# Attention with an MLP behind it on one core: tail exponentials added to the row sums by accumulating transfers, the sums' product half a pair later with half its passes

## The chip, the cores and the metric

One core of a Trainium2 chip runs the whole kernel. The metric is the device time of one execution in microseconds, as the median of several runs. Engines are TensorE (PE, its weight loads PEld), VectorE (DVE), ScalarE (ACT), GpSimd (POOL) and SyncE (SP); DMA transfers are issued by SP and by POOL.

## What is computed

```python
# q, k, v: (4 batches, 12 heads, 448 positions, 64); w_in (768, 2048), w_out (2048, 768)
scores = cap * np.tanh(np.matmul(q, k.transpose(0, 1, 3, 2)) / sqrt(64) / cap)
attn = np.exp(scores - scores.max(axis=-1, keepdims=True))
attn = attn / (np.sum(attn, axis=-1, keepdims=True) + 1e-09)
x = heads side by side of np.matmul(attn, v)          # (1792, 768)
h = x @ w_in
P = a[0] + a[1] * h + a[2] * h * h + a[3] * h * h * h
Q = 1.0 + abs(b[0]) * abs(h) + abs(b[1]) * h * h
out = (P / (Q + 1e-6)) @ w_out
```

## The kernel before

**Steps and pairs.** Attention goes through 24 steps p, each with two heads (j = 0, 1) of one batch; two steps make a pair k. The 448 keys of a head are cut in four blocks n: three of 128 and a tail of 64. Scores stand transposed, keys in partitions and the 448 queries in columns. For n = 0, 1, 2 a tile holds both heads side by side (128 x 896). The two tails share one tile of 128 x 448: keys of the first head in partitions 0 to 63, of the second in 64 to 127. A step takes the blocks in the order 0, 1, 3, 2 (ORDER, line 56); m counts places in this order.

**What a step does.** `scores` (L417, and L316 for the tail) multiplies keys by queries into one of three PSUM tiles ps. ScalarE applies tanh in place (L429) and then the exponential (L449) into an SBUF tile: e for n < 3, et for the tail. The cap is bounded here, so no maximum is subtracted (the flag `bounded`; the other branch does not run). VectorE adds the three e tiles into es[p], first block 1, then block 2 (L455). At place m = 2 TensorE also transposes keys (into the PSUM bank mi, L335 and L337) and queries (L341) of step p + 2, and VectorE turns them into high and low halves (`convert_k`, L369 and L370; L361 and L364). The value product `pv` (L500) of step p - 1 comes in two parts: blocks 0 and 1 at m = 2 of step p, block 2 and the tail at m = 3. VectorE copies its result to U[p - 1] (L509).

**The sums' product.** `norm(k)` (L512 to L551) makes the sums over keys for the four heads of a pair: a product of a 128 x 32 block of ones with es, for each of two heads of two steps, then four more products that add the tails. A tail tile holds two heads, so its stationary operand is `half[j]`, ones in the 64 partitions of head j and zeros elsewhere:

```python
        for last in range(2):
            for j in range(2):
                for x in range(2):
                    h = 32 * (2 * j + x)
                    st, mv = (self.half[j], tails[x][0][:, 0]) if last else (self.ones, es[x][:, j])
```

The result stands in mi. VectorE copies it to DB (L533), four transfers put it in a tile of 32 x 56, VectorE adds the guard and takes the reciprocal (L542, L543), one transfer writes it to DRAM (dn), and two broadcast it over 128 partitions. `xout` (L562) multiplies U by it. All these transfers are GpSimd's except for the last pair, where they are SyncE's. `norm(p // 2 - 1)` is called at the end of m = 3 of each even step.

**What sets the order.** `Plan` collects operations with estimated costs (D_NS, line 58, is that of the sums' product) and what they read and write, and `flush` writes each engine's queue in the order in which they would start by these costs. Each engine works through its queue in order.

**Behind attention.** `split_x` turns six pieces of x (kc) in two halves m into a high and a low part. For m = 1 both are ScalarE's (L573, L579), and a transfer by GpSimd accumulates x on the low one. The MLP has stage 1 (L755, x times w_in, three products for each piece), a rational function on ScalarE and VectorE (L782 to L795, whose high and low halves are L794 and L795) and stage 2 (L820). The first two units of stage 1 need the pieces of m = 0 alone; the third and fourth need those of m = 1, which depend on the last steps' outputs.

## Time and profile before

| | |
|---|---|
| median of three runs (lowest, highest) | 699.83 us (698.43, 700.53) |
| the profiled execution: its time | 696.99 us |
| the profiled execution: span of the core | 695.2 us |
| mean granted clock of TensorE | 0.995 |
| busy: PE, PEld, DVE, ACT, POOL | 674.9, 545.4, 552.1, 450.1, 102.3 us |

A span runs from the first to the last instruction. Busy time is that of one engine's instructions; a busy TensorE need not be at its peak, as its matmuls are pipelined. A wait is put down to the engine whose signal came last. One fp32 product of TensorE shows as two records.

### The profile page before, as it was taken

The numbers are of one execution on the slowest core, as the hardware profiler recorded it, in microseconds if no ns is written. First come the engines' busy times: TensorE is split into PE (matmuls) and PEld (weight loads), VectorE is DVE, ScalarE is ACT, GpSimd is POOL, SyncE is SP. The second block draws the span as 40 slices with busy tenths as digits, with TensorE's granted clock in tenths as the row PEclk, the third lists the DMA queues.
The fourth block names the chain that finished last, engine by engine and source line by source line (L and its number), as shares of the span: only waits on it lengthen the run. The fifth ranks groups of instructions, "written<-read, shape, count | busy, mean of one in ns | idle before, by whom it ended". The sixth has DMA issues, their size and how long they took to land.

```text
span 695.2 us, 9792 instructions
## 1 busy us (share of the span) xinstructions
PE 674.9 (97%) x3781; PEld 545.4 (78%) x3781; DVE 552.1 (79%) x682; ACT 450.1 (65%) x551; POOL 102.3 (15%) x168
## 2 busy tenths in 40 slices
PE   6899999999999899999999999999999999999986
PEld 4554455445547799999999999999999999999986
DVE  4579998987864879767998688698689869778783
ACT  3788878888895796666557458546655744755520
POOL 4022232333222200011002001101100200110000
PEclk9999999999999999999999999999999999999999
DMA  6637666744224744267119316714821841681044
GB/s 147 144 97 208 173 144 130 166 108 109 55 74 81 132 143 153 66 135 140 46 51 170 76 51 153 137 45 89 185 68 45 146 106 46 137 206 67 23 180 166
DMA packets 81912, 79.95 MB, mean 115 GB/s; under 512 B 48960, under 2 KB 69184, under 8 KB 81856
## 3 DMA queue, kind: packets, MB, share of 16 engines
q1 hardware_dynamic: 70496, 53.74, 26.3%
q0 software_dynamic: 11360, 25.50, 20.6%
q8 instruction: 31, 0.51, 0.3%
q14 instruction: 25, 0.20, 0.1%
HBM read 50.73 MB, written 25.65 MB: 110 GB/s over the span
## 4 chain that ended last, share of the span: by engine, by line
PE 85%; DVE 5%; ACT 5%; DMA 2%; SPq 2%; issue 1%; DVEq 0%
PE ps L755 32%; PE ps L820 16%; PE pv L500 9%; PE mi L820 8%; PE pv L820 8%; PE ps L417 6%; PE mi L528 3%; PE ps L316 2%; ACT etiles L449 2%; ACT ps L429 2%; SPq L283 1%; PE ps L341 1%; PE mi L335 1%; DMA arena_r<-dn 1%; DVE arena_f L455 1%
## 5 line engine op out<-in xcount | busy, mean ns | idle before, releaser
L755 PE MATMUL ps<-arena_r,ring 128*128 128x512 f32 (+1 forms) x1152 | 249.2, 368 | 2.0 <-DMA arena_r<-arena_f 1.5
L755 PEld LDWEIGHTS ps<-arena_r,ring 128*128 128x128 f32 x1152 | 209.0, 188 | 28.7 <-DMA arena_r<-arena_f 1.9
L429 ACT ACTIVATE ps<-ps 128x896 f32<-128x896 f32 (+1 forms) x96 | 76.6, 817 | 33.2 <-PE ps L417 28.2
L820 PE MATMUL ps<-arena_r,etiles 128*128 128x384 f32 x462 | 90.3, 335 | 0.7 <-DVE etiles L795 0.7
L786 DVE SCALAR_TENSOR_TENSOR arena_f<-arena_f,bab 128x896 f32<-128x896 f32 x32 | 36.8, 1150 | 63.9 <-ACT arena_f L783 63.9
L782 ACT ACTIVATE arena_f<-ps,b 128x896 f32<-128x896 f32 x32 | 32.4, 1013 | 84.5 <-PE ps L755 84.3
L283 POOL DMA_DIRECT2D sums<-arena_f x42 | 36.5, 869 | 341.8 <-ACT arena_f L852 340.5
L820 PEld LDWEIGHTS ps<-arena_r,etiles 128*128 128x128 f32 x462 | 81.1, 188 | 2.2 <-DVE etiles L795 1.0
L449 ACT ACTIVATE etiles<-ps,acap 128x896 f32<-128x896 f32 (+1 forms) x84 | 77.9, 959 | 1.5 <-DVE arena_r L361 0.5
L820 PE MATMUL pv<-arena_r,etiles 128*128 128x384 f32 x231 | 77.1, 335 | 0.0
L820 PE MATMUL mi<-arena_r,etiles 128*128 128x384 f32 x231 | 76.8, 334 | 0.0
L794 ACT CAST etiles<-arena_f 128x896 fp32r<-128x896 f32 x32 | 30.3, 945 | 66.6 <-DVE arena_f L793 66.6
L417 PEld LDWEIGHTS ps<-arena_r 64*128 64x128 f32 x432 | 37.6, 189 | 39.4 <-ACT etiles L449 15.1
L500 PE MATMUL pv<-etiles,ring 128*64 128x448 f32 x312 | 68.1, 553 | 0.0
L417 PE MATMUL ps<-arena_r 64*128 64x448 f32 x432 | 59.1, 394 | 3.2 <-DVE arena_r L370 1.7
L820 PEld LDWEIGHTS pv<-arena_r,etiles 128*128 128x128 f32 x231 | 43.3, 188 | 1.2
L791 DVE SCALAR_TENSOR_TENSOR arena_f<-arena_f,one 128x896 f32<-128x896 f32 x32 | 36.8, 1149 | 9.2 <-ACT arena_f L789 9.2
L820 PEld LDWEIGHTS mi<-arena_r,etiles 128*128 128x128 f32 x231 | 43.4, 188 | 0.0
L820 PE MATMUL ps<-ring,etiles 128*128 128x384 f32 x210 | 42.2, 335 | 0.8 <-DVE arena_f L849 0.8
L500 PEld LDWEIGHTS pv<-etiles,ring 128*64 128x64 f32 x312 | 18.6, 136 | 26.3 <-issue 23.0
L820 PEld LDWEIGHTS ps<-ring,etiles 128*128 128x128 f32 x210 | 37.0, 188 | 1.6 <-DVE arena_f L849 1.1
L790 DVE SCALAR_TENSOR_TENSOR arena_f<-arena_f,a,ps 128x896 f32<-128x896 f32 x32 | 36.6, 1143 | 0.6
(114 smaller groups left out, 1066.6 us busy)
## 6 DMA issues: line engine op xcount, KB each, us to landing
sums<-arena_f POOLq DMA_DIRECT2D x42, 384.0 KB, 5.7
arena_f<-in_moe_w_out_dram SPq DMA_DIRECT2D x16, 768.0 KB, 4.0
arena_f<-in_moe_w_in_dram SPq DMA_DIRECT2D x16, 768.0 KB, 7.1
out_dram<-arena_f SPq DMA_DIRECT2D x13, 384.0 KB, 2.6
ring<-in_q_dram SPq DMA_DIRECT2D x44, 112.0 KB, 3.9
arena_r<-dn POOLq DMA_DIRECT2D x22, 224.0 KB, 3.7
ring<-in_k_dram SPq DMA_DIRECT2D x33, 128.0 KB, 3.2
ring<-in_v_dram SPq DMA_DIRECT2D x11, 384.0 KB, 4.3
```

The source lines that it names most:

```text
L283: self.op(eng, (625 if local else 450) if eng == SP else 1050, lambda: e.dma_start(out, in_, **accum), r, w, nbytes=nbytes, **kw)
L417: m = nc.tensor.matmul(self.PS[i][:, j, 0:448], st[r], mv[r], start=y == 0, stop=y == 2)
L429: self.op(ACT, act_ns(448 * w, True), lambda: nc.scalar.activation(ps, ps, AF.Tanh), ["table"], [("ps", i), ("psb", i)])
L449: self.op(ACT, act_ns(448 * w, sk[0][0] == "ps", 1), lambda: nc.scalar.activation(e, src, AF.Exp, scale=acap), sk + ["table"], [ek])
L500: m = nc.tensor.matmul(self.PV[64 * j:64 * j + 64, 0:448], st, mv, start=c == 0, stop=c == 3)
L755: r = nc.tensor.matmul(po[:, ts], w[:, y, kc], x, start=kc == 0 and z == 0, stop=kc == KC - 1 and z == 2)
L782: self.op(ACT, act_ns(n, True, 1), lambda: T.activation(Bt, h, AF.Abs, scale=b[:, 0:1]), hk, bk)
L786: self.op(DVE, dve_ns(n, 1), lambda: stt(Bt, C, bab[:, 1:2], Bt, ALU.mult, ALU.add), ck + ["bab"], bk)
L790: self.op(DVE, dve_ns(n, 1), lambda: stt(A, A, a[:, 1:2], h, ALU.add, ALU.mult), hk, ak)
L791: self.op(DVE, dve_ns(n, 1), lambda: stt(Bt, Bt, one, C, ALU.add, ALU.mult), ck, bk)
L794: self.op(ACT, act_ns(n, False), lambda: T.copy(GH(), A), ak, K("gh", ig) + first)
L820: r = nc.tensor.matmul(po[n][:, 0:384], st, mv[:, 384 * n:384 * n + 384], start=(y == 0 and x == 0), stop=(y == self.NCH - 1 and x == 2))
```

## The change

The tail's exponentials no longer go through TensorE for the sums. `add_tail` adds them to es in SBUF: for each head j a transfer issued by GpSimd accumulates 64 x 448 floats of et on the same partitions of es. It is called behind the addition of block 2; in the last step VectorE does it with two additions. The keys of es are cut in two, one for each head. The sums' product keeps the four products with ones alone. `norm` is called at m = 2 of odd steps. There are four es tiles in place of three, and two et tiles in place of four; the blocks `half` go, with their memsets. D_NS is halved.

```diff
-D_NS = 1520
+D_NS = 760
...
         if n == 3:
-            i = p % len(self.et32) if self.bounded else p % 2
+            i = p % len(self.et32) if self.bounded else 0
...
-        es, ks = self.es[p % 3], [("es", p % 3)]
+        es, ks = self.es[p % 4], [("es", p % 4, j) for j in range(2)]
         a, ak = self.etile(p, 0) if n == 1 else (es, None)
         self.op(DVE, dve_ns(896), lambda: nc.vector.tensor_tensor(es, a, e, ALU.add), [ek] + [ak] * (n == 1), ks)
+        if n == 2 and (not self.bounded or p + 1 < self.B * self.NP):
+            self.add_tail(p, POOL)
+
+    def add_tail(self, p, eng):
+
+        es = self.es[p % 4]
+        t, tk = self.etile(p, 3)
+        for j in range(2):
+            o, i = (x[64 * j:64 * j + 64] for x in (es[:, j], t[:, 0]))
+            if eng == POOL:
+                self.dma(POOL, o, i, [tk], [("es", p % 4, j)], accum_op=ALU.add)
+            else:
+                self.op(DVE, dve_ns(448), lambda o=o, i=i: self.nc.vector.tensor_tensor(o, o, i, ALU.add), [tk],
+                        [("es", p % 4, j)])
...
         def sums():
-            for last in range(2):
-                for j in range(2):
-                    for x in range(2):
-                        h = 32 * (2 * j + x)
-                        st, mv = (self.half[j], tails[x][0][:, 0]) if last else (self.ones, es[x][:, j])
-                        m = nc.tensor.matmul(D[h:h + 32], st, mv, start=not last, stop=last == 1)
+            for j in range(2):
+                for x in range(2):
+                    h = 32 * (2 * j + x)
+                    m = nc.tensor.matmul(D[h:h + 32], self.ones, es[x][:, j], start=True, stop=True)
...
                 if self.bounded and m > 1 and p:
                     self.pv(p - 1, m - 2)
-                    if m == 3 and p % 2 == 0:
+                    if m == 2 and p % 2 and p > 2:
                         norm(p // 2 - 1)
...
             self.pv(P1 - 1, 0)
+            self.add_tail(P1 - 1, DVE)
             self.pv(P1 - 1, 1)
             norm(P1 // 2 - 1)
```

Lines behind `add_tail` move: L500 is L514 in the changed kernel, L509 is L523, L528 is L539, L533 is L544, L542 and L543 are L553 and L554, L562 is L573, L755 is L766, L782 to L795 are L793 to L806, L820 is L831.

TensorE's queue in the middle of attention, before: an even step from its scores to the sums' product and the odd step's first scores (arena_r holds queries and keys, mi the transposes and the sums).

```order
L417 MATMUL ps_131<-arena_r 128x448 x6
L417 MATMUL ps_132<-arena_r 128x448 x6
L316 MATMUL ps_130<-arena_r 128x448 x3
L335 MATMUL mi<-ident,ring_150 128x128 x3
L337 MATMUL mi<-ident,ring_150 128x128
L341 MATMUL ps_130<-ident,ring_150 128x112 x4
L500 MATMUL pv<-etiles,ring_150 64x448 x4
L417 MATMUL ps_131<-arena_r 128x448 x6
L500 MATMUL pv<-etiles,ring_150 64x448 x2
L500 MATMUL pv<-arena_f,ring_150 64x448 x2
L528 MATMUL mi<-arena_f 32x448 x8
L417 MATMUL ps_132<-arena_r 128x448 x6
```

And the changed kernel there, from the odd step's transposes on:

```order
L335 MATMUL mi<-ident,ring_151 128x128 x3
L337 MATMUL mi<-ident,ring_151 128x128
L341 MATMUL ps_132<-ident,ring_151 128x112 x4
L514 MATMUL pv<-etiles,ring_150 64x448 x4
L539 MATMUL mi<-arena_f 32x448
L539 MATMUL mi<-etiles,arena_f 32x448
L539 MATMUL mi<-arena_f 32x448
L539 MATMUL mi<-etiles,arena_f 32x448
L417 MATMUL ps_130<-arena_r 128x448 x6
L514 MATMUL pv<-etiles,ring_150 64x448 x2
L514 MATMUL pv<-arena_f,ring_150 64x448 x2
```

The product of eight became one of four, and it moved from behind both parts of an even step's value product to between the two parts of an odd step's, next behind the transposes into the same bank.

GpSimd's queue over one pair, before (in order: reciprocals to DRAM, their broadcast, tails of v, the four small transfers of the sums):

```order
L283 DMA dn<-arena_f 32x56
L283 DMA arena_r<-dn 64x896 x2
L283 DMA ring_150<-in_v_dram 64x2x64 x2
L283 DMA arena_f<-arena_f 8x1x56 x4
L283 DMA dn<-arena_f 32x56
```

And in the changed kernel, where transfers of 64x448 are the new ones:

```order
L283 DMA dn<-arena_f 32x56
L283 DMA ring_150<-in_v_dram 64x2x64 x2
L283 DMA arena_f<-arena_f 64x448
L283 DMA arena_r<-dn 64x896 x2
L283 DMA arena_f<-arena_f 64x448
L283 DMA arena_f<-arena_f 8x1x56 x4
L283 DMA etiles<-arena_f 64x448 x2
L283 DMA dn<-arena_f 32x56
```

Four accumulating transfers joined each pair: an even step's stand around the broadcast, an odd step's between the four small transfers and the reciprocals.

VectorE's queue behind attention, before (L562 is the output's multiplication, L786 to L793 the rational function of a unit, L795 its low half, L705 a step of making a weight):

```order
L790 SCALAR_TENSOR_TENSOR arena_f<-arena_f,a,ps_130 128x896
L791 SCALAR_TENSOR_TENSOR arena_f<-arena_f,one 128x896
L792 SCALAR_TENSOR_TENSOR arena_f<-arena_f,a 128x896
L562 TENSOR_TENSOR arena_f<-arena_r,arena_f 128x448
L793 SCALAR_TENSOR_TENSOR arena_f<-arena_f 128x896
L562 TENSOR_TENSOR arena_f<-arena_r,arena_f 128x448
L786 SCALAR_TENSOR_TENSOR arena_f<-arena_f,bab 128x896
L795 TENSOR_TENSOR etiles<-arena_f,etiles 128x896
```

And in the changed kernel:

```order
L801 SCALAR_TENSOR_TENSOR arena_f<-arena_f,a,ps_130 128x896
L802 SCALAR_TENSOR_TENSOR arena_f<-arena_f,one 128x896
L573 TENSOR_TENSOR arena_f<-arena_r,arena_f 128x448 x2
L803 SCALAR_TENSOR_TENSOR arena_f<-arena_f,a 128x896
L716 TENSOR_SCALAR arena_f<-arena_f 128x768
L804 SCALAR_TENSOR_TENSOR arena_f<-arena_f 128x896
L573 TENSOR_TENSOR arena_f<-arena_r,arena_f 128x448 x2
L797 SCALAR_TENSOR_TENSOR arena_f<-arena_f,bab 128x896
L806 TENSOR_TENSOR etiles<-arena_f,etiles 128x896
```

All four multiplications of the last two pairs' outputs and one step of a weight now stand inside the first unit's chain. On TensorE the third piece of the third unit (L766) moved from ahead of stage 2's first products (L831) to behind them.

## Rows read from the trace of the kernel before

**Rows 1.** The page: busy time of the engines, and the last chain by line

```profile
PE 674.9 (97%) x3781; PEld 545.4 (78%) x3781; DVE 552.1 (79%) x682; ACT 450.1 (65%) x551; POOL 102.3 (15%) x168
...
PE ps L755 32%; PE ps L820 16%; PE pv L500 9%; PE mi L820 8%; PE pv L820 8%; PE ps L417 6%; PE mi L528 3%; PE ps L316 2%; ACT etiles L449 2%; ACT ps L429 2%; SPq L283 1%; PE ps L341 1%; PE mi L335 1%; DMA arena_r<-dn 1%; DVE arena_f L455 1%
```

**Rows 2.** Stretches: from:to, length, busy PE PEld DVE ACT POOL, clock, DMA

```profile
36.81:52.77 15.96, 15.96 (x109) 8.22 (x107) 12.14 (x17) 13.01 (x17) 3.61 (x7) 1.00 0.42 119
52.77:69.67 16.90, 16.19 (x108) 8.17 (x106) 16.29 (x25) 15.17 (x20) 4.79 (x9) 1.00 0.75 205
69.67:86.23 16.56, 16.23 (x108) 8.19 (x106) 15.84 (x24) 14.82 (x20) 4.77 (x9) 1.00 0.62 165
86.23:102.19 15.96, 15.96 (x109) 8.22 (x107) 15.20 (x24) 13.42 (x17) 5.12 (x9) 1.00 0.58 138
102.19:118.59 16.40, 16.02 (x109) 8.21 (x107) 13.41 (x20) 14.14 (x19) 4.77 (x9) 1.00 0.55 125
118.59:135.44 16.85, 16.08 (x109) 8.14 (x107) 15.53 (x23) 14.31 (x19) 4.79 (x9) 1.00 0.74 161
135.44:152.27 16.83, 16.06 (x109) 8.13 (x107) 14.90 (x22) 14.34 (x19) 4.78 (x9) 1.00 0.53 124
152.27:168.24 15.97, 15.97 (x109) 8.25 (x107) 13.35 (x20) 13.20 (x17) 4.80 (x9) 1.00 0.47 113
168.24:184.19 15.95, 15.95 (x109) 8.21 (x107) 13.00 (x19) 13.00 (x17) 4.78 (x9) 1.00 0.31 78
184.19:199.34 15.15, 15.15 (x101) 7.31 (x99) 10.46 (x15) 12.29 (x16) 4.80 (x9) 1.00 0.20 59
```

**Rows 3.** Waits from 0 to 240 us: who for whom: total, times, longest

```profile
ACT ps L429 <- PE ps L417: 28.2, 23, 5.0
```

**Rows 4.** Timeline of PE around one sums' product: start, length, instruction

```profile
118.59 0.96 PE L528 MATMUL mi<-arena_f 128*32 128x448 f32 x8
119.36 0.94 PE L528 MATMUL mi<-etiles,arena_f 128*32 128x448 f32 x8
120.23 1.08 PE L417 MATMUL ps<-arena_r 64*128 64x448 f32 x8
```

**Rows 5.** Timeline where the product will stand; last row: L533's shortest, median, longest ns

```profile
156.68 0.69 DVE L369 CAST arena_r<-mi 128x512 fp32r<-128x512 f32 x1 [0.94 <-PE mi L337]
157.41 0.69 DVE L370 TENSOR_TENSOR arena_r<-mi,arena_r 128x512 fp32r<-128x512 f32 x1
158.62 0.88 PE L417 MATMUL ps<-arena_r 64*128 64x448 f32 x6
...
59.12 0.87 PE L417 MATMUL ps<-arena_r 64*128 64x448 f32 x6
59.85 0.68 DVE L370 TENSOR_TENSOR arena_r<-mi,arena_r 128x512 fp32r<-128x512 f32 x1
...
L533 DVE COPY arena_f<-mi x12: 605/624/625, 38.6 to 213.7; 128x448 f32<-128x448 f32 x12
```

**Rows 6.** GpSimd's transfers: issue time (shortest, median, longest ns); then us to landing

```profile
L283 POOL DMA_DIRECT2D arena_f<-arena_f x44: 497/514/543, 39.5 to 203.8; - x44
L283 POOL DMA_DIRECT2D arena_r<-arena_f x2: 1217/1244/1272, 209.2 to 213.2; - x2
...
arena_r<-arena_f POOLq DMA_DIRECT2D x6, 448.0 KB, 4.8
arena_f<-arena_f POOLq DMA_DIRECT2D x44, 1.8 KB, 2.4
```

**Rows 7.** Timeline of PE behind attention, with its waits

```profile
231.58 1.09 PE L755 MATMUL ps<-arena_r,ring 128*128 128x512 f32 x4 [1.48 <-DMA arena_r<-arena_f]
...
234.09 0.62 PE L820 MATMUL ps<-arena_r,etiles 128*128 128x384 f32 x2 [0.65 <-DVE etiles L795]
...
236.27 0.91 PE L755 MATMUL ps<-arena_r,ring 128*128 128x512 f32 x3 [0.51 <-DVE arena_f L790]
```

**Rows 8.** Line L455 (additions of tiles): shortest, median, longest ns

```profile
L455 DVE TENSOR_TENSOR arena_f<-etiles x24: 1016/1092/1097, 15.4 to 205.4; 128x896 f32<-128x896 f32 x24
```

More of the change, by code (lines that the diff above doesn't have):

```diff
@@ L462, in exp_shifted @@
         tail = tail[:, 0]
-        m, mk = self.et32[2][:, 0], [("et", 2)]
+        m, mk = self.et32[1][:, 0], [("et", 1)]
         ma, mak = self.U[p], [("u0", p), ("u1", p)]
@@ L518, in norm @@
         D, DB, sc, dn = self.MI[:, 0:448], self.DB, self.SC[k % 2], self.dn[k % 2]
-        es = [self.es[(2 * k + x) % 3] for x in range(2)]
-        tails = [self.etile(2 * k + x, 3) for x in range(2)]
+        es = [self.es[(2 * k + x) % 4] for x in range(2)]
         def sums():
-            for last in range(2):
-                for j in range(2):
-                    for x in range(2):
-                        h = 32 * (2 * j + x)
-                        st, mv = (self.half[j], tails[x][0][:, 0]) if last else (self.ones, es[x][:, j])
-                        m = nc.tensor.matmul(D[h:h + 32], st, mv, start=not last, stop=last == 1)
+            for j in range(2):
+                for x in range(2):
+                    h = 32 * (2 * j + x)
+                    m = nc.tensor.matmul(D[h:h + 32], self.ones, es[x][:, j], start=True, stop=True)
             return m
-        self.op(PE, D_NS + TURN_NS, sums, [("es", (2 * k + x) % 3) for x in range(2)] + [t[1] for t in tails] + ["ones"],
+        self.op(PE, D_NS + TURN_NS, sums, [("es", (2 * k + x) % 4, j) for x in range(2) for j in range(2)] + ["ones"],
                 ["mi", "turn"])
@@ L590, in attention @@
                     self.op(POOL, 300, fn, [], [(key, n)])
-        for t, x in [(self.ones, 1.0)] + [(self.half[j][64 * y:64 * y + 64], float(j == y)) for j in range(2) for y in range(2)]:
-            self.op(POOL, 150, lambda t=t, x=x: nc.gpsimd.memset(t, x), [], ["ones"])
+        self.op(POOL, 150, lambda: nc.gpsimd.memset(self.ones, 1.0), [], ["ones"])
         self.prep_qk(0)
@@ L776, in rational @@
         GH, GL = (lambda x=x: self.G[ig]()[:, x].rearrange("p (a b) -> p a b", a=2) for x in range(2))
-        first = [("e", n) for n in range(NE)] + [("et", n) for n in (2, 3)] if u == 0 else []
+        first = [("e", n) for n in range(NE)] + [("es", 3, j) for j in range(2)] if u == 0 else []
         V, T = nc.vector, nc.scalar
@@ L991, in memory @@
                 t, o = take(w)
-                keys("A", o, ((nm, n), w))
+                keys("A", o, ([(nm, n, j) for j in range(2)] if nm == "es" else (nm, n), w))
                 l.append(t.rearrange("p (a b) -> p a b", b=448))
@@ L998, in memory @@
             self.e.append(self.etiles[:, 896 * n:896 * n + 896].rearrange("p (a b) -> p a b", b=448))
-        for n in range(2):
-            o = 896 * NE + 448 * n
-            keys("A", 3 * 10 ** 6 + 4 * o, (("et", len(self.et32)), 448))
-            self.et32.append(self.etiles[:, o:o + 448].rearrange("p (a b) -> p a b", b=448))
-        t, o = take(96)
-        keys("A", o, ("ones", 96))
-        self.ones, *self.half = (t[:, 32 * x:32 * x + 32] for x in range(3))
+        o = 896 * NE
+        keys("A", 3 * 10 ** 6 + 4 * o, ([("es", 3, j) for j in range(2)], 896))
+        self.es.append(self.etiles[:, o:o + 896].rearrange("p (a b) -> p a b", b=448))
+        self.ones, o = take(32)
+        keys("A", o, ("ones", 32))
         for n in range(2):
```

## Prediction

> **What bounds the kernel now.** I read the busy times and the chain first, then one table of stretches, then the places where the sums' product stands. TensorE is busy for 97% of the span, and the chain that ended last runs mostly through its lines; the sums' product (L528) holds 3% of that chain, some 20 us [rows 1]. So a pass taken out of TensorE's order is worth its time where nothing else is about to end later.
>
> The stretches from the start of one sums' product to the start of the next show where that holds [rows 2]. Nine of them, from 36.81 to 184.19 us, hold one pair of steps each, 147.38 us together. Four last 15.95 to 15.97 us, and in these TensorE is busy for every microsecond: 15.96 is the bare work. The other five are longer by 0.94, 0.60, 0.44, 0.89 and 0.87 us, 3.74 together. VectorE explains two of them: it is busy for 16.29 of 16.90 us and 15.84 of 16.56 us, and for 15.20 of 15.96 in the next; the early weights are made there. The tenth stretch has no transposes and is all TensorE, 15.15.
>
> ScalarE waited 28.2 us for scores [rows 3]: it starves while the sums' product runs. It has room, and is fed earlier when that product shrinks.
>
> **Passes removed.** One sums' product runs from 118.59 to 120.23, 1.64 us: the first set (ones by the sums, 8 records) holds 0.77 of it, the second (half-ones by the tails, 8 records) 0.87 [rows 4]. The second set goes. I take half, 0.82 us; the ends over 12 products are 9.2 and 10.4 us.
>
> Stretch by stretch: a pair can't be shorter than TensorE's 15.96 - 0.82 = 15.14, nor than VectorE's work, which stays as it is (the copy of the sums, the reciprocals, all additions of the tiles). The greater of the two gives 15.14, 16.29, 15.84, 15.20, 15.14, 15.53, 15.14, 15.14 and 15.14: a gain of 0.82, 0.61, 0.72, 0.76, 1.26, 1.32, 1.69, 0.83 and 0.81, 8.8 us. That is the upper end; it has the present stalls vanish. The lower end gives the three stretches with a full VectorE nothing and the other six 0.82 each: 4.9. I take the middle, **6.9 us**: the stalls should shrink, since ScalarE is fed earlier, but the product's new place brings a wait, next. The tenth stretch gives 0.82 more: **0.8**.
>
> **The move.** The product used to follow both halves of the value product, in an even step. Now it stands between the halves in the odd step after it, right behind the transposes of the keys, and both use the bank mi. So it has to wait until VectorE has read the transposes out (L369, L370). In a calm stretch that costs nothing: L369 began at 156.68 after 0.94 us of idling, and L370 ended at 157.41 + 0.69 = 158.10 [rows 5]. TensorE was through the first half of the value product at 158.62, and will be 1.64 us earlier, at 156.98, as the old product no longer stands ahead; but VectorE moves up too, by its idle 0.94 and by the 0.62 of the copy L533 that stood ahead of it [rows 5], 1.56 in all, to 156.54. No wait. Where VectorE is full it costs: L370 ended at 59.85 + 0.68 = 60.53, TensorE would be there at 59.12 - 1.64 = 57.48, and of the 3.05 us between them the missing copy takes off 0.62: a wait of 2.4 us. Then it is VectorE's order that sets the stretch, which is why I left those three at half of what their VectorE time allows.
>
> Everything behind the product is half a pair later: the copy, the four small transfers, the reciprocal, the broadcast, the multiplication of the outputs. In the middle of attention their readers are a whole pair away, so I cost this at nothing.
>
> **The transfers added.** There are 46, each adding 64 x 448 floats (112 KB) to the sums; the last step's two additions are VectorE's. The trace of before has no such transfer of this size. Below it lie the 1.8 KB copies: 0.51 us of GpSimd's time each, landed after 2.4 us; above it the 448 KB accumulating ones: 1.24 and 4.8 us [rows 6]. GpSimd is busy for 4.8 us of a stretch [rows 2]; four more issues make that 6.9 to 9.8 us of 15.1. It fits. The sums of the odd step are read a whole step later, some 7 us, and those of the even step later still, so a landing of 2.4 to 4.8 us is hidden. One half in each even step stands behind the two broadcast transfers on GpSimd's queue, which wait for the reciprocals' transfer; its readers are the product nearly two pairs later and ScalarE's next tail in the same buffer, one pair later (the buffers go from four to two). That cover is a whole stretch; gone, each microsecond too late would stop ScalarE and then TensorE. I price the transfers at nothing. The two additions on VectorE at the end take about 0.62 each, by the copy of the same width [rows 5]; TensorE has six more products of the first unit ahead of the last sums' product meanwhile, so nothing too.
>
> **The end of attention.** Here I expect a loss. The last two products save 1.64 us more, but the next to last now stands much nearer the last, and its broadcast feeds pieces of x that TensorE needs soon after. Before, TensorE waited there 1.48 us for an accumulating transfer, 0.65 for VectorE's low half of the first unit and 0.51 for VectorE again [rows 7]. In the new order the third piece of x goes behind the first products of the second stage, and VectorE's chain for the first unit has one more output multiplication and a step of the weights ahead of its end. So TensorE comes 1.64 earlier to data that comes no earlier, with less work to fill the time. Ends: both gains kept, +1.6, or waits as large again as those now there, -2.6. I take **-1.0**, nearer to the waits, as the order puts work ahead of what is waited for.
>
> **Sum.** 6.9 + 0.8 - 1.0 = 6.7 us. The profiled execution took 696.99 us (span 695.2), which is 2.84 below the median of the runs, 699.83; 696.99 - 6.7 = 690.3, and against the median **693.1 us**. By the ends of my own terms it is 11.2 us (688.6) to 3.1 us (696.7). A measurement of this kernel can tell about 0.3%, 2.1 us, from no change.
>
> **Rivals.** *The wait takes the gain's place.* In the three full stretches the new wait of 2.4 us outweighs the 1.64 that came off ahead of it, -0.8 each, and the end of attention costs its full 2.6. The rest gives 4.9 + 0.8. That leaves 0.7 us: 699.1. For it speaks rows 5, against it that the present stalls of those stretches are paid out of the same lateness, and fall as the new wait rises.
>
> *GpSimd's issues hold up VectorE: slower.* If VectorE's additions of two tiles in SBUF stood still while GpSimd issues, four issues of 0.51 us add at least 2.06 us to VectorE in each pair. The stretches become 15.14, 18.35, 17.90, 17.26, 15.47, 17.59, 16.96, 15.41 and 15.14, 149.2 us, 1.8 more than now; with the 0.8 of the tenth and the -1.0 this is 2.0 us slower, 701.8. It decides from about 1.8 us of standstill in each pair. Against it: the 24 first additions L455 lasted 1016 to 1097 ns [rows 8], though GpSimd issued in the same stretches. The Trainium skill, SBUF — State Buffer, section "SBUF: two separate sides", says that VectorE and GpSimd share one pair of ports under an exclusive lock, which an operation of VectorE with two SBUF inputs can lose to a GpSimd operation that reads SBUF. By that rule the time would be the 701.8; the trace shows no such stretching in L455.
>
> *All stalls vanish.* VectorE's slack is used fully and the end of attention keeps its gain: 688.6. For it speaks that the stalls follow ScalarE's starving; against it that VectorE works already 95% of three stretches (47.33 of 49.42 us).
>
> That the passes are not halved is no rival: the order lists four products instead of eight.
>
> **Chances.** Forecast 0.67, wait in place of the gain 0.15, VectorE held up 0.11, all stalls gone 0.07. Faster by over 0.3%: the first and the last, 0.74; within: 0.15; slower: 0.11. The range 689.0 to 699.5 holds the forecast nearly whole and the first rival, and leaves out the slower one and the best.
>
> **What would show it.** L528's successor has 96 records instead of 192, 0.8 us a set; the calm stretches last 15.1 us with TensorE busy throughout; in the full ones TensorE waits for L370 ahead of the product; the new transfers are issued in 0.5 to 1.2 us and L455 keeps its 1.09; ScalarE's wait for scores falls well below 28 us; the waits at 231 to 236 us grow. I am wrong if the calm stretches are not shorter, if ScalarE or TensorE waits for an accumulating transfer in attention, or if L455 lengthens.

## The result, and the profile after

The changed kernel takes 708.84 us (median of four runs, 707.28 to 711.75) against 699.13 us for the kernel before in the same comparison: 1.0147 times, with an interval of 1.0118 to 1.0176. I had forecast 693.1 us. The profiled execution took 711.75 us, the slowest of the four; its span is 710.0 us, 14.8 longer than before. By the medians the change costs 9.7 us, so about 5 of the 14.8 belong to these two executions and not to the kernels.

The page of the changed kernel (busy times; granted clock of TensorE in 40 slices; the last chain by line), which answers to [rows 1]:

```profile
PE 677.5 (95%) x3685; PEld 548.0 (77%) x3685; DVE 552.8 (78%) x684; ACT 450.7 (63%) x551; POOL 141.7 (20%) x210
...
PEclk9699899999999999999999999999999999999999
...
PE ps L766 30%; PE ps L831 15%; PE mi L831 8%; PE pv L831 8%; PE pv L514 5%; DMA arena_r<-dn 4%; PE ps L417 3%; DMA arena_f<-arena_f 2%; DVE arena_f L455 2%; PE ps L316 1%; SPq L283 1%; DMA arena_r<-arena_f 1%; PE mi L539 1%; POOL arena_f L283 1%; DVE arena_r L361 1%
```

TensorE lost 96 records and yet was busy for longer: part of its time it ran at a lower clock. The broadcast of the reciprocals (arena_r<-dn) has 4% of the chain; it had 1%.

The stretches from one sums' product to the next (columns as in [rows 2]), six of the nine and their sum:

```profile
43.68:59.55 15.87, 15.31 (x101) 7.99 (x99) 12.79 (x20) 13.62 (x18) 8.26 (x13) 1.00 0.81 180
59.55:80.71 21.16, 18.33 (x99) 9.66 (x99) 18.11 (x28) 16.98 (x22) 8.09 (x14) 0.84 0.99 207
...
98.30:115.94 17.64, 15.53 (x99) 7.92 (x99) 11.90 (x19) 12.46 (x15) 7.67 (x13) 1.00 0.85 152
115.94:135.95 20.01, 17.09 (x101) 9.00 (x99) 15.61 (x23) 15.05 (x19) 8.86 (x14) 0.91 0.67 123
...
171.22:187.54 16.32, 15.45 (x99) 7.92 (x99) 13.01 (x20) 13.45 (x17) 7.86 (x13) 1.00 0.75 134
187.54:202.74 15.20, 15.20 (x100) 7.97 (x98) 12.54 (x20) 12.83 (x16) 7.49 (x12) 1.00 0.51 93
sum 159.06, PE 143.64 PEld 74.12 DVE 129.02 ACT 125.92 POOL 73.07; mean PE 15.96 PEld 8.24 DVE 14.34 ACT 13.99 POOL 8.12
```

Nine pairs take 159.06 us; they took 147.38 [rows 2]. Only the last of them is near what I forecast (15.14): 15.20 us with TensorE busy throughout. The stretch 98.30 to 115.94 shows the fault best: VectorE works for 11.90 us, ScalarE for 12.46, TensorE for 15.53, and 17.64 pass.

VectorE in that stretch (start, length, instruction, the idle time ahead of it and what ended it):

```profile
98.87 0.68 DVE L364 SCALAR_TENSOR_TENSOR arena_r<-ps,c,arena_r 128x448 fp32r<-128x448 f32 x1
99.47 0.61 DVE L544 COPY arena_f<-mi 128x448 f32<-128x448 f32 x1
104.80 0.63 DVE L573 TENSOR_TENSOR arena_f<-arena_r,arena_f 128x448 f32<-128x448 f32 x1 [4.71 <-DMA arena_r<-dn]
105.34 0.62 DVE L523 COPY arena_f<-pv 128x448 f32<-128x448 f32 x1
```

VectorE stands for 4.71 us at the output's multiplication L573, until the broadcast is there; the copy L523 behind it could have run, and TensorE's next value product waits for L523 (1.27 us at 106.01). The waits from 0 to 240 us, as in [rows 3]:

```profile
ACT ps L429 <- PE ps L417: 33.1, 33, 4.7
...
DVE arena_f L573 <- DMA arena_r<-dn: 16.2, 7, 4.7
```

ScalarE starves more than before, not less. Before, VectorE waited 7.8 us for the broadcast, all but 0.3 of it behind the middle of attention. From 40 to 210 us, before:

```profile
DVE arena_f L562 <- DMA arena_r<-dn: 0.3, 1, 0.3
```

Now it is 16.2, all of it between 40 and 210 us. From 40 to 200 us TensorE waited 13 times for VectorE's or ScalarE's results, 15.2 us in all; before, 3.0. TensorE's scores around the longest of these waits, 2.83 us:

```profile
70.05 0.86 PE L417 MATMUL ps<-arena_r 64*128 64x448 f32 x6
73.74 1.49 PE L417 MATMUL ps<-arena_r 64*128 64x448 f32 x6 [2.83 <-DVE arena_r L364]
```

Two-microsecond stretches around it (columns as in [rows 2]):

```profile
66.00:68.00 2.00, 2.00 (x13) 0.81 (x14) 0.00 (x0) 2.00 (x3) 1.33 (x2) 1.00 1.11 280
...
70.00:72.00 2.00, 0.91 (x8) 0.48 (x6) 2.00 (x4) 1.97 (x3) 0.63 (x1) 1.00 1.21 200
72.00:74.00 2.00, 0.26 (x2) 0.29 (x4) 1.97 (x5) 0.14 (x1) 0.61 (x2) 0.79 1.14 222
74.00:76.00 2.00, 2.00 (x8) 1.40 (x8) 2.00 (x4) 1.51 (x2) 0.51 (x1) 0.50 0.42 95
76.00:78.00 2.00, 2.00 (x10) 1.71 (x9) 2.00 (x3) 2.00 (x4) 0.00 (x0) 0.50 0.95 292
78.00:80.00 2.00, 2.00 (x8) 0.77 (x8) 1.64 (x4) 1.82 (x3) 1.57 (x3) 0.50 0.34 88
80.00:82.00 2.00, 2.00 (x16) 0.55 (x14) 2.00 (x4) 0.00 (x0) 1.22 (x2) 1.00 0.86 145
```

From 66 to 68 VectorE does nothing; three microseconds later TensorE runs dry, and from 74 to 80 it is granted 0.50 of its clock, 1.2 GHz. So the pair of 21.16 us lost time to the clock on top of the wait: the passes from 73.74 to 80.71 took 6.97 us, where the same ones took 4.08 at full clock (3.28 from 64.31 to 67.59 and 0.80 for the scores from there), some 2.9 us. The kernel before had 1.00 in every stretch of [rows 2].

### The profile page after: what moved, and what is told of

Its sections match the earlier page's. It is cut to its first block, busy times and chain, and to the rows that moved or that the text cites. A ratio compares the mean times of both kernels' runs of the same rounds, so it can differ in the third digit from the quotient of the medians.

```text
span 710.0 us, 9722 instructions
## 1 busy us (share of the span) xinstructions
PE 677.5 (95%) x3685; PEld 548.0 (77%) x3685; DVE 552.8 (78%) x684; ACT 450.7 (63%) x551; POOL 141.7 (20%) x210
## 4 chain that ended last, share of the span: by engine, by line
PE 74%; DMA 8%; DVE 8%; issue 3%; ACT 3%; SPq 1%; POOL 1%; DVEq 0%; ACTq 0%; POOLq 0%
PE ps L766 30%; PE ps L831 15%; PE mi L831 8%; PE pv L831 8%; PE pv L514 5%; DMA arena_r<-dn 4%; PE ps L417 3%; DMA arena_f<-arena_f 2%; DVE arena_f L455 2%; PE ps L316 1%; SPq L283 1%; DMA arena_r<-arena_f 1%; PE mi L539 1%; POOL arena_f L283 1%; DVE arena_r L361 1%
## 5 line engine op out<-in xcount | busy, mean ns | idle before, releaser
L766 PE MATMUL ps<-arena_r,ring 128*128 128x512 f32 (+1 forms) x1152 | 250.0, 368 | 1.7 <-DMA arena_r<-arena_f 1.4
L766 PEld LDWEIGHTS ps<-arena_r,ring 128*128 128x128 f32 x1152 | 208.9, 188 | 29.3 <-DMA arena_r<-arena_f 2.3
L831 PE MATMUL ps<-arena_r,etiles 128*128 128x384 f32 x462 | 91.0, 337 | 2.1 <-ACT etiles L805 2.1
L793 ACT ACTIVATE arena_f<-ps,b 128x896 f32<-128x896 f32 x32 | 32.3, 1009 | 83.3 <-PE ps L766 83.3
L831 PEld LDWEIGHTS ps<-arena_r,etiles 128*128 128x128 f32 x462 | 81.8, 189 | 3.8 <-ACT etiles L805 2.5
L831 PE MATMUL pv<-arena_r,etiles 128*128 128x384 f32 x231 | 77.4, 337 | 0.0
L831 PE MATMUL mi<-arena_r,etiles 128*128 128x384 f32 x231 | 77.2, 336 | 0.0
L417 PE MATMUL ps<-arena_r 64*128 64x448 f32 x432 | 61.3, 401 | 10.8 <-DVE arena_r L364 9.1
L449 ACT ACTIVATE etiles<-ps,acap 128x896 f32<-128x896 f32 x72 | 70.2, 1010 | 0.7
L283 POOL DMA_DIRECT2D arena_f<-arena_f x80 | 55.2, 746 | 76.8 <-DVE arena_f L455 55.0
L514 PE MATMUL pv<-etiles,ring 128*64 128x448 f32 x264 | 60.2, 565 | 1.3 <-DVE arena_f L523 1.3
L831 PEld LDWEIGHTS pv<-arena_r,etiles 128*128 128x128 f32 x231 | 43.7, 189 | 1.2
L831 PEld LDWEIGHTS mi<-arena_r,etiles 128*128 128x128 f32 x231 | 43.7, 189 | 0.0
L831 PE MATMUL ps<-ring,etiles 128*128 128x384 f32 x210 | 42.2, 335 | 0.8 <-DVE arena_f L860 0.8
L831 PEld LDWEIGHTS ps<-ring,etiles 128*128 128x128 f32 x210 | 37.0, 188 | 1.6 <-DVE arena_f L860 1.1
```

The source lines that it names most:

```text
L283: self.op(eng, (625 if local else 450) if eng == SP else 1050, lambda: e.dma_start(out, in_, **accum), r, w, nbytes=nbytes, **kw)
L417: m = nc.tensor.matmul(self.PS[i][:, j, 0:448], st[r], mv[r], start=y == 0, stop=y == 2)
L449: self.op(ACT, act_ns(448 * w, sk[0][0] == "ps", 1), lambda: nc.scalar.activation(e, src, AF.Exp, scale=acap), sk + ["table"], [ek])
L514: m = nc.tensor.matmul(self.PV[64 * j:64 * j + 64, 0:448], st, mv, start=c == 0, stop=c == 3)
L766: r = nc.tensor.matmul(po[:, ts], w[:, y, kc], x, start=kc == 0 and z == 0, stop=kc == KC - 1 and z == 2)
L793: self.op(ACT, act_ns(n, True, 1), lambda: T.activation(Bt, h, AF.Abs, scale=b[:, 0:1]), hk, bk)
```

## The experiments

Each kernel was compared with runs of the kernel before on the same chip; the ratios are against those (their medians lie between 698.28 and 699.29 us). For the place of a loss, two stretches are read from the profiled execution of each: from the tail's scores (L316) of step 3 to those of step 21, nine pairs, and from those of step 23 to the end of the span. One execution stands for a kernel there, and it can lie up to 4.8 us from the kernel's median (behind both halves: 704.74 against 699.95); so a difference of a few microseconds between two stretches is no more than an indication.

| kernel | median us | ratio to before | steps 3 to 21 | step 23 to end |
|---|---|---|---|---|
| before | 699.13 | | 147.4 | 492.8 |
| changed | 708.84 | 1.0147 (1.0118 to 1.0176) | 159.1 | 496.1 |
| passes only, old place | 693.46 | 0.9925 (0.9896 to 0.9954) | 143.6 | 491.9 |
| moved, no transfers | 706.42 | 1.0108 (1.0083 to 1.0134) | 155.8 | 497.9 |
| changed, additions on VectorE | 711.23 | 1.0177 (1.0130 to 1.0224) | 158.8 | 496.5 |
| changed, landings planned later | 707.64 | 1.0131 (1.0098 to 1.0164) | 148.3 | 501.9 |
| changed, product at the old place | 707.58 | 1.0119 (1.0085 to 1.0154) | 156.8 | 491.4 |
| changed, behind both halves | 699.95 | 1.0022 (1.0005 to 1.0039) | 144.6 | 502.4 |
| moved, no transfers, loads later | 702.69 | 1.0053 (1.0034 to 1.0071) | 149.3 | 497.0 |
| old place, landings planned later | 708.47 | 1.0145 (1.0118 to 1.0172) | 150.2 | 500.8 |
| behind both halves, pair 10 early | 705.57 | 1.0099 (1.0076 to 1.0121) | 142.4 | 501.6 |
| the same, its chain on SyncE | 703.95 | 1.0076 (1.0059 to 1.0092) | 142.8 | 502.0 |
| behind both halves, no transfers | 696.86 | 0.9965 (0.9948 to 0.9982) | 140.7 | 499.7 |
| behind both, pairs 9 to 11 at old place | 700.81 | 1.0035 (1.0017 to 1.0053) | 145.4 | 497.7 |
| the same, last additions on VectorE | 697.52 | 0.9999 (0.9978 to 1.0020) | 143.7 | 495.9 |
| pairs 8 to 11 so | 695.85 | 0.9971 (0.9954 to 0.9987) | 147.4 | 493.7 |
| moved, no transfers, broadcast planned later | 705.08 | 1.0093 (1.0077 to 1.0110) | 148.1 | 501.3 |
| changed, broadcast planned later | 707.22 | 1.0121 (1.0087 to 1.0154) | 151.1 | 501.6 |

In most kernels with half the passes, what steps 3 to 21 take beyond some 139 us is TensorE's waits plus half of its time at 1.2 GHz. With these taken off, 138.7 us are left of the changed kernel's 159.1 (waits 15.2, clock 5.1), 139.4 with the passes alone (4.2, none), 138.5 where the product was moved without transfers (13.9, 3.4) and 138.0 behind both halves (4.9, 1.7); over all of them it is 137.6 to 141.6.

**Passes alone.** Of the kernel before:

```diff
-            for last in range(2):
+            for last in range(1):
...
-D_NS = 1520
+D_NS = 760
```

> The kernel before with the tails' four passes left out of the sums' product, at its old place, no transfers (the sums lack the tails). Both theories: the passes alone are worth what I priced them at, pairs of 15.1 to 15.3 us in the middle of attention, 689 to 693 us in all. If the passes were hidden by something else all along, it stays within 2 us of 699.

693.46 us, half a microsecond above the range. The pairs without a stall take 15.21 us, against 15.96, so a product's passes are worth about what they were priced at. But the nine pairs gained only 3.8 us (143.6 against 147.4), less than my lower end of 4.9: four stalls of TensorE remain there, 4.2 us, the longest 1.99 for the queries' low halves (L364).

**Moved, without transfers.** Of the changed kernel:

```diff
-        if n == 2 and (not self.bounded or p + 1 < self.B * self.NP):
+        if n == 2 and not self.bounded:
             self.add_tail(p, POOL)
...
-            self.add_tail(P1 - 1, DVE)
```

> The changed kernel without the accumulating transfers and without the last step's two additions (the sums lack the tails). Theory (the transfers on GpSimd's queue make the reciprocals' chain land late, and VectorE, working in order, stands at the output's multiplication until the broadcast is there): 689 to 694 us, VectorE waits under 3 us for the broadcast, which lands after 3.7 us again. Rival (the product's new place, behind the transposes in the same bank, and the chain half a pair later are the cause): 704 us or more, with TensorE still waiting for VectorE.

My first theory fell: 706.42 us without a single accumulating transfer, 13 us more than with the passes gone at the old place. This kernel leaves the tails out of the sums. VectorE still stood at the broadcast, and the product waited in its bank (waits from 40 to 210 us):

```profile
DVE arena_f L573 <- DMA arena_r<-dn: 12.6, 4, 4.4
...
PE mi L539 <- DVE arena_r L370: 3.8, 3, 1.7
```

**Additions on VectorE.** `self.add_tail(p, DVE)` in every step.

> The changed kernel with VectorE doing all the tails' additions (four of 128-partition-wide tiles' halves in a pair, some 0.55 us each) in place of the transfers. Theory: the broadcast lands after 3.7 us again, VectorE's wait for it is gone, but VectorE has 2.2 us more in each pair: full in all of them, 700 to 705 us. Rival (the new place): as slow as the changed kernel or slower, 709 to 716.

711.23 us: the rival's number. VectorE's wait for the broadcast did fall, to 2.3 us from 40 to 210 us, as the theory had it; but the additions cost VectorE some 22 us from 40 to 200, and TensorE's wait for L370 ahead of the product was 9.5 us in eight waits, more than in the two kernels above. The wait in the bank goes with the place.

**Landings planned later.** The planner's `flush` gives each of GpSimd's transfers 1.5 us to land; here four kinds get a figure of their own:

```diff
-                d0 = max(self.free[e] + (850 if e == SP else 1500), self.dma_free)
+                d0 = max(self.free[e] + o["lag"], self.dma_free)
```

> The changed kernel with nothing but the planner's figures changed: the time it allows for the landing of GpSimd's transfers goes from 1.5 us to 4.5 (sums' small transfers), 2.5 (reciprocals), 5.0 (broadcast) and 2.5 (accumulating), so that VectorE's order puts reciprocals and output multiplications later. Theory: VectorE's 16.2 us of waiting for the broadcast falls under 4, TensorE's clock stays up in attention, 692 to 699 us. Rival (the transfers cost by themselves, through slower landing of everything or held ports, wherever VectorE's order puts the readers): 705 us or more.

In time the rival is right (707.64), in mid attention the theory: steps 3 to 21 fall from 159.1 to 148.3 us, and VectorE no longer waits for the broadcast there. Now TensorE waits for the transposes' read-out L370 ahead of the product, 7.9 us in five waits, and what follows step 23 is 5.8 us longer.

**Product at the old place, with transfers.**

```diff
-                    if m == 2 and p % 2 and p > 2:
+                    if m == 3 and p % 2 == 0:
```

> The changed kernel with the sums' product back at the end of the even step, behind both halves of the value product: accumulating transfers and half the passes, old place. My first theory has fallen with the kernel that was moved without transfers. Theory now (the product's new place is the main cause: its chain of small transfers meets the loads of keys and queries, and the product waits for the transposes' read-out in its bank): 692 to 700 us, VectorE's wait for the broadcast under 4 us, no wait for L370 ahead of the product; a wait of TensorE for the odd step's last accumulating transfer is possible, up to 1 us in each pair. Rival (the transfers hold up GpSimd's queue wherever the product stands): 704 us or more.

Wrong: 707.58. The wait for L370 is gone, but VectorE stands at the broadcast, and TensorE then twice for 5 us (67.80 and 90.58) at queries that VectorE reads out soon behind it (waits from 40 to 210 us):

```profile
DVE arena_f L573 <- DMA arena_r<-dn: 10.9, 5, 3.7
...
PE ps L417 <- DVE arena_r L364: 10.1, 2, 5.1
```

The loss lies in these two pairs, of 22.59 and 23.30 us. The end, 491.4, is as good as with the passes alone. At this place it is the transfers that cost, 13 us from step 3 to 21 (156.8 against 143.6). GpSimd's chain lands later: its 1.8 KB copies after 6.3 us, against 4.0 without the large transfers at the same place, and the broadcast after 6.2 against 4.2 (medians, 40 to 180 us). The two kernels also differ in the number of es and et tiles, which no kernel tests by itself. TensorE waits once for an accumulating transfer, 0.96 us.

**Behind both halves, same odd step.** `m == 3` in place of `m == 2`.

> The changed kernel with the product in the same odd step, but behind both halves of the value product instead of between them, some 4 us away from the transposes. Theory of the bank (TensorE's wait for L370 is what the place costs): the waits for L370 ahead of the product vanish and 697 to 702 us remain. Theory of the chain (it is half a pair late and meets the loads): VectorE still waits for the broadcast and the time stays at 703 to 709.

699.95 us, as the theory of the bank has it. Waits from 40 to 210 us:

```profile
DVE arena_f L573 <- DMA arena_r<-dn: 3.9, 3, 2.5
...
ACT arena_f L449 <- DMA arena_f<-arena_f: 2.5, 1, 2.5
...
PE mi L539 <- DVE arena_r L370: 1.0, 1, 1.0
```

TensorE waits once for L370 ahead of a product. But VectorE's wait for the broadcast fell as well, which that theory does not explain. The second line is a tail's exponential that waits until an accumulating transfer has read its buffer; the pair with it takes 19.00 us, where six take 15.21 to 15.23. This one edit is worth 8.9 us in the median, with all transfers in place, and steps 3 to 21 take 144.6 us: the fault in mid attention is the place between the halves. What was gained is in part given back behind step 23: 502.4 us, 9.6 more than before.

**Loads half a pair later**, in the moved kernel without transfers:

```diff
-                step = 4 * (p % 2) + m
-                if step < 5:
-                    self.load(p // 2 + 2, [("scores", p, n)], step, 5)
+                if p % 2:
+                    self.load(p // 2 + 2, [("scores", p, n)], m, 4)
```

> The kernel that was moved without transfers (its sums lack the tails), with the loads of keys and queries issued in the odd step, half a pair later, in four parts. Theory of the collision: reciprocals and broadcast land as at the old place, in under 2.5 and under 4.5 us at the longest in most pairs, VectorE's wait for the broadcast falls from 12.6 us to under 4, and 694 to 701 us remain. Rival (order or bank alone): landing times and waits as before, 704 to 708. Risk: the loads may now come late for the transposes themselves.

At 702.69 us both sides missed, and it does not settle the collision. The wait for the broadcast fell to 1.5 us, but the broadcast itself landed later (5.7 us in the median, 4.7 in the kernel it was made from); the planner had put L573 later as well. TensorE now waits 3.9 us for queries.

**Old place, landings planned later.** The edits of those two kernels together.

> Product at its old place with transfers, and the planner's landing figures at 4.5, 2.5, 5.0 and 2.5 us as in the kernel with planned landings. If VectorE's order is what is left to mend, 1 to 4 us faster than the old place with the planner's old figures: 690 to 697. If the order does not matter at the old place, the same within 2 us; the end of attention can lose, as the planned landings did there before.

Wrong again: 708.47. Steps 3 to 21 gain 6.6 us over the planner's old figures, the end loses 9.4.

**Behind both halves, the next to last product early.**

```diff
-                    if m == 2 and p % 2 and p > 2:
+                    if m == 3 and (p + 2 == P1 if p + 3 > P1 else p % 2 and p > 2):
```

> The product behind both halves in the odd step, with transfers, but the next to last product back in step 22, as in the kernel before. In the kernel with all products behind both halves, the steps 3 to 21 took 144.6 us (before: 147.4), and all from step 21 to the end 516.7 (before: 508.0). Theory (the next to last product stands too near the last, and its outputs come too late for the second half of x): the end is 507 to 510 again, and 693 to 697 us in all, faster than both kernels. Rival (accumulating transfers ahead of the last chain on GpSimd's queue hold the end): 513 or more from step 21 on, and 699 to 702.

705.57: the end stayed at 501.6. My theory of the end fell. TensorE's first product of stage 2 waited 5.09 us for ScalarE's high half of the first unit. ScalarE had been idle for 4.91 us at 207 to 212, waiting for outputs of pair 9, which the kernel before had multiplied by 204.8.

**That product's chain on SyncE.** `q = SP if k + 2 >= self.B * self.NP // 2 else POOL`.

> As the one with the next to last product in step 22, and that product's small transfers, reciprocals and broadcast issued by SyncE instead of GpSimd (as the last one's are). Theory (early product is enough): within 1.5 us of that kernel. Rival (GpSimd's queue is what holds the end): 2 to 5 us faster than that kernel.

703.95, and the end not shorter (502.0): in the profiled executions the 1.6 us lie ahead of step 3, where the edit changes nothing. GpSimd's queue isn't what holds the end there.

**Behind both halves, no transfers.** The edits of the two kernels so named, together; the sums lack the tails.

> The product behind both halves in the odd step without any of the transfers and without the last step's additions (the sums lack the tails). It prices the transfers at this place, against the 699.95 us and the 144.6 us for the steps 3 to 21 with them. Theory (the place between the halves was the fault, the transfers cost little): steps 3 to 21 take 143.5 to 145, and the whole is 0 to 3 us faster. Rival (transfers cost by slower landing in the queue): 4 us or more faster.

696.86 us, 3.1 below the same place with transfers: that is their price there, between theory and rival. The nine pairs, 140.7, came out below the theory's range. The end is 499.7 even so: the late chain holds most of it, not the transfers.

**The last three pairs at the old place**, and then also the last tails on VectorE:

```diff
-                    if m == 2 and p % 2 and p > 2:
+                    if m == 3 and (p % 2 and 2 < p < 20 or p % 2 == 0 and p >= 20):
...
-            self.add_tail(p, POOL)
+            self.add_tail(p, POOL if p < 18 else DVE)
```

> Product behind both halves in the odd step up to pair 8; for the last three pairs (9, 10 and 11) where the kernel before has it. My theory that the next to last product alone holds the end has fallen: with it in step 22 the end stayed long, because ScalarE's first two pieces of the second half of x wait for the outputs of pair 9, which were then a step late. Theory: with pair 9 back in step 20 the stretch from the tail product of step 23 to the end falls from 501.6 to 493 to 497 us; a wait of TensorE for an accumulating transfer ahead of the products of pairs 9 and 10 costs 1 to 3: 695 to 700 in all. Rival (GpSimd's queue holds the end whatever the order): 702 to 706.

> As the one with the last three pairs at the old place, and the tails of the steps from 18 on added by VectorE, so that no product waits for an accumulating transfer there and GpSimd's queue is free for the last chains. Theory: 1 to 4 us faster than that one, 692 to 698, faster than the kernel before. Rival (VectorE, with 2.2 us more in each of these pairs, is late for the first unit instead): no gain, or slower.

> The same split one pair earlier: pairs 8 to 11 at the old place, tails from step 16 on added by VectorE. If VectorE's share is what decides, it loses 0.5 to 2 us against the split at pair 9; if the lateness of the last chains decides, it gains as much.

700.81, 697.52 and 695.85 us; the end shrinks to 497.7, 495.9 and 493.7. The order of the last chains holds most of the end, then, and the last transfers some of the rest. The last version (borders at 18 and 16) pays 18.04 and 18.97 us for two pairs with VectorE's additions. **695.85 us is faster than both kernels**: 0.9971 of before (0.9954 to 0.9987), a small gain, and the best of many versions. Where it comes from no trace shows: its profiled execution, 697.56 us, has 147.4 from step 3 to 21 and 493.7 behind, no better than before's.

**VectorE's order.** One planner's figure, the broadcast's landing, 5.0 us in place of 1.5, in the kernel without transfers and in the changed one. TensorE's order stays the same up to 220 us; VectorE's output multiplications go back a few places, and some of ScalarE's instructions shift with them:

> The kernel that was moved without transfers (product between the halves, sums lack the tails), with one planner's figure changed: the landing it allows for the broadcast is 5.0 us in place of 1.5, so that VectorE's order puts the output's multiplications some two to four instructions later; TensorE's order stays word for word. Theory (VectorE stands in its order at a broadcast that lands later than planned): its wait for the broadcast falls from 12.6 us to under 3, steps 3 to 21 from 155.8 us to 143 to 149, and the time from 706.4 to 694 to 701. Rival (the bank that the product shares with the transposes is the fault): waits for L370 stay or grow, steps 3 to 21 stay above 152, 703 us or more.

> The changed kernel with that one figure (broadcast 5.0 us in place of 1.5) and nothing else. Theory: steps 3 to 21 fall from 159.1 us to 147 to 153 and the time from 708.8 to 698 to 704. Rival (transfers, or the bank): above 155 and 705 or more.

In mid attention both came out as the theory says. Waits from 40 to 210 us of the first:

```profile
PE mi L539 <- DVE arena_r L370: 5.2, 6, 2.0
...
DVE arena_f L573 <- DMA arena_r<-dn: 0.3, 1, 0.3
```

155.8 became 148.1, and 159.1 became 151.1: 7.7 and 8.0 us are VectorE standing, in its fixed order, ahead of a broadcast that lands later than planned. They are TensorE's waits (13.9 to 8.1 us, and 15.2 to 10.0) and its clock (mean granted in these steps 0.978 to 0.988, and 0.968 to 0.989). What is left over the place behind both halves (140.7 without transfers) is 7.4 us, and the waits for L370, 5.2, are the largest thing that the profile shows in it; they grew from 3.8, as the rival has it. In total time the theory missed, by 4.1 and 3.2 us above its upper ends (705.08, 707.22), as the rivals had it: the later order again lengthens the end, by 3.4 and 5.6. The medians fell by 1.3 and 1.6 us, so the size of the effect, unlike its sign, rests on one execution of each kernel.

## Why the prediction was wrong

**Passes removed: right in the product, too hopeful for nine pairs.** The second set went, and a product takes some 0.89 us (59.55 to the next scores at 60.44) where it took 1.64: 0.75 in place of the 0.82 I took. Where nothing waits, a pair is 15.20 to 15.25 us, forecast 15.14. My sum had 6.9 us from step 3 to 21, with stalls that shrink. At the old place, with the passes alone, they did not all shrink: 3.8 us. Behind both halves without transfers it is 6.6 us. So what I added up was there to be had, at another place and with sums that lack the tails.

**The move: the step that failed.** I wrote that everything behind the product is half a pair later, that "their readers are a whole pair away", and costed it at nothing. The reader's distance in the program was not what counted. L573 stands in VectorE's queue where the planner expects its data, and the planner allows 1.5 us for a landing. Moved by half a pair, L573 fell ahead of the value product's copy and block 2's addition, and its broadcast was not there. That is 7.7 of the 12.2 us that the move costs from step 3 to 21 (155.8 against 143.6), by the kernel with the later order, in one execution of each. That the place is at fault is firmer: with the product behind both halves the medians fall from 708.84 to 699.95 us, and without transfers from 706.42 to 696.86.

**The wait in the bank: seen, and not only where VectorE is full.** The first rival's mechanism is there, but not as what costs most: 0.56 and 1.68 us ahead of two products in the changed kernel. With VectorE's waits for the broadcast gone it is 5.2 us in the kernel without transfers, 7.9 with all landings planned later. I had 2.4 us in each of three full stretches and none in calm ones; in the first of these kernels it is 0.55, 0.94 and 2.02 early, and 0.53 to 0.62 in each of three pairs behind 120 us. That VectorE's other waits hide it in the changed kernel is argued, not shown.

**The transfers: the second step that failed.** I priced them at nothing. Their cover (the readers' distance) held: no engine waits for their data in mid attention. But they share GpSimd's queue with the chain of the sums. The changed kernel, from 30 to 200 us (transfer, size, median us to landing), and below it the kernel before, from 40 to 180 us:

```profile
arena_r<-dn POOLq DMA_DIRECT2D x16, 224.0 KB, 6.8
arena_f<-arena_f POOLq DMA_DIRECT2D x28, 112.0 KB, 3.9
...
arena_f<-arena_f POOLq DMA_DIRECT2D x36, 1.8 KB, 5.5
dn<-arena_f POOLq DMA_DIRECT2D x9, 7.0 KB, 3.4
```

```profile
arena_r<-dn POOLq DMA_DIRECT2D x16, 224.0 KB, 3.7
...
arena_f<-arena_f POOLq DMA_DIRECT2D x36, 1.8 KB, 2.9
...
dn<-arena_f POOLq DMA_DIRECT2D x9, 7.0 KB, 1.7
```

Not all of this is the transfers': without them, but moved, the reciprocals take 3.7 us and the broadcast 4.7 (40 to 180 us).

And the accumulating transfers stand in the order around it:

```profile
110.78 0.54 POOL L283 DMA_DIRECT2D dn<-arena_f  x1 [1.84 <-DVE arena_f L554]
111.35 1.21 POOL L283 DMA_DIRECT2D ring<-in_v_dram  x2
113.54 0.87 POOL L283 DMA_DIRECT2D arena_f<-arena_f  x1 [0.98 <-DVE arena_f L455]
114.60 1.07 POOL L283 DMA_DIRECT2D arena_r<-dn  x2 [0.19 <-issue]
115.64 0.91 POOL L283 DMA_DIRECT2D arena_f<-arena_f  x1
```

The broadcast goes out behind an accumulating transfer that waited for VectorE, and ahead of another. The price is 3.1 us in all behind both halves, 2.4 between them (708.84 against 706.42), and 14.1 at the old place (707.58 against 693.46), 13 of them from step 3 to 21. Behind both halves the cover itself fails once, ScalarE's 2.51 us. Their own landing, 3.9 us, lies between my two ends.

**VectorE held up by GpSimd's issues: the sign right, the mechanism absent.** The additions L455 keep their time (shortest, median, longest ns), as in [rows 8]:

```profile
L455 DVE TENSOR_TENSOR arena_f<-etiles x18: 1069/1083/1093, 15.1 to 210.6; 128x896 f32<-128x896 f32 x18
```

The Trainium skill, SBUF — State Buffer, section "SBUF: two separate sides", led me to this rival; the trace shows no lock in which VectorE loses to the issue of a transfer, with GpSimd's busy time up from 102.3 to 141.7 us. The section speaks of GpSimd operations that read SBUF, and nothing here shows VectorE's additions beside such an operation, so its rule stands untested.

**TensorE's clock: not in the sum at all.** The mean granted clock fell from 0.995 to 0.979. About half of the fall lies ahead of step 3 (0.83 against 0.96), where it hardly counts: with the passes alone it is 0.83 there too, and step 3 comes no later (39.73 us against 39.88). In the nine pairs two stretches are at 0.84 and 0.91: TensorE had 1.2 GHz from 73.2 to 80.0 and from 131.2 to 134.6 us, which costs at most half of these times, 3.4 and 1.7 us. Ahead of each TensorE had been idle, for 2.83 us once and for 1.95 and 0.97 together. A third lies behind attention, from 243.8 to 247.2 us, after a wait of 2.08.

**The end of attention: right in sign, at my lower end.** From the tail's scores of step 21 to the end of the span it is 507.9 before and 510.5 after: -2.6, where I took -1.0 with ends at +1.6 and -2.6. The wait for the accumulating transfer was 1.42 us, and the one for stage 2 moved to ScalarE:

```profile
243.82 2.29 PE L831 MATMUL ps<-arena_r,etiles 128*128 128x384 f32 x6 [2.08 <-ACT etiles L805]
248.03 8.39 PE L766 MATMUL ps<-arena_r,ring 128*128 128x512 f32 x38 [0.30 <-DVE arena_f L801]
257.84 1.08 PE L766 MATMUL ps<-arena_r,ring 128*128 128x512 f32 x4 [1.42 <-DMA arena_r<-arena_f]
```

**Added up:** -0.5 up to step 3, -11.7 in nine pairs, -2.6 from step 21 on, 14.8 us of span, in two executions whose kernels differ by 9.7 us in the median.

What stays open: how much of the move's other part is the bank and how much the order of the rest, and whether the loads of keys and queries make the chain land later at the new place (the reciprocals took 3.7 us there without any accumulating transfer, 1.6 at the old place).

## What to carry to other kernels

Where engines work in a fixed order, a step that is moved must be followed to the place at which its last reader stands in its engine's queue: compare the landing times of the trace with those the order was planned by, and name what is queued behind that reader. Price a transfer not only by its own cover but by what shares its queue, and price a stall of TensorE of some 3 us with the lower clock that followed it here. When a change has a good half, look for another place for it: the change that cost 1.5% with the product between the halves costs 0.2% with it behind them, and gains 0.3% with the last four chains left where they were and the last tails added by VectorE.

## What the runs showed of the hardware

The clock that follows a stall was the surprise. TensorE, idle from 70.9 to 73.7 us, had 1.2 GHz until 80.0, and six passes of scores took 1.49 us instead of 0.86; the stall of 2.83 us cost some 2.9 more. From 80 on it had 2.4 GHz again, having worked without a wait in between. The Trainium skill, TensorE: Matmul & The Clock Gate, section "What's actually happening", says that the clock is half after idling and full after sustained work; the trace agrees.

At each of three places the small transfers landed later when the large ones shared their queue. The 1.8 KB copies (medians, 40 to 180 us) took 2.7 us without the accumulating transfers and 4.1 with them behind both halves, 3.8 and 5.7 between the halves, 4.0 and 6.3 at the old place. What else the kernels do counts for as much: with all transfers, but landings planned later, they took 3.1 us, and in the kernel before 2.9. The Trainium skill, DMA: Bandwidth & Descriptors, section "SWDGE vs HWDGE vs iDMA", says that all transfers from GpSimd share one queue; the trace agrees in that much, with one queue of the software kind (q0) in both profiles.
